# K and V of a batch in one 2 MB load each, in an attention kernel with grouped heads

## The chip, the cores and the metric

The kernel runs on one core of a Trainium2 chip. The metric is the device time of one execution in microseconds. The core's engines are TensorE (PE in the profile; PEld is its loading of weights), VectorE (DVE), ScalarE (ACT), GpSimd (POOL) and SyncE (SP). Each runs its own instructions in order, and they meet through semaphores. Loads from HBM into the on-chip memory (SBUF) are carried by 16 DMA engines; a load is given to them by one instruction on the queue of POOL or SP.

## The reference, cut to what matters

```python
B, Sq, D = 32, 4, 1024
Hq, Hkv, Sk, Dh = 32, 4, 2048, 128          # all bfloat16
q = (x @ wq).reshape(B, Sq, Hq, Dh).transpose(0, 2, 1, 3)
k = repeat(k_cache, 8, axis=1)               # k_cache, v_cache: [B, Hkv, Sk, Dh]
v = repeat(v_cache, 8, axis=1)
scores = einsum("bhqd,bhkd->bhqk", q, k) * Dh ** -0.5
o = einsum("bhqk,bhkd->bhqd", softmax(scores), v)
return o.transpose(0, 2, 1, 3).reshape(B, Sq, Hq * Dh) @ wo
```

Each batch has 2 MB of K and 2 MB of V (four groups of 512 KB each), and wq and wo are 8 MB each, so 151 MB are read in all. The 4 query rows of the 32 heads make 128 rows per batch, 32 for each group of heads that shares a K and a V.

## The kernel before, in words

All loads but that of x go through one ring of nine slots in SBUF, each of 2 MB (128 partitions by 16 KB). The order of the loads is the list `stream` (line 123): four slots of wq, K of batches 0 to 2, then V of batch b and K of batch b+3 in turn, at the end four slots of wo. POOL issues them in that order (lines 151 to 167, through `fetch`, line 144). Before it issues load n it waits until load n-9 has been used up (`freed`, line 133): a wq slot by its last projection matmul, a K slot by its last transposes, a V slot by its last PV matmul. Each slot is filled by four DMAs of 512 KB, each with a semaphore of its own; for K and V these are the four groups of heads. In a group, partition p holds 16 consecutive rows of the cache, which is one piece of 4 KB.

The work on a batch i goes through these steps; the line numbers are those of the profile:

- `kt` (line 236, copied out at lines 346 on DVE and 348 on ACT): K is transposed by TensorE, 64 transposes in eight fills f = 0 to 7 of eight transposes, two fills for each group. A fill goes to one of four PSUM buffers (ps_a, ps_b, ps_c, ps_o, in turn), waits for the load of its group g = f // 2 and for the buffer to have been copied out. DVE copies out five of the fills, ACT three.
- `qk` (line 281): 16 matmuls give the scores of 128 rows by 2048 keys.
- max and its negative (lines 372 and 373, DVE), exp with the row sums (line 401, ACT), the reciprocal `rinv` and a diagonal matrix of it (lines 381 and 382, DVE). On DVE, rinv and diag stand between the third and the fourth copy of the `kt` fills.
- `tr` (line 252): four fills of four matmuls transpose the probabilities and scale them by the diagonal; they use the same four PSUM buffers.
- `pv` (line 263): 64 matmuls with V; it waits for all four parts of V. Its result is copied out on DVE (`ot`, line 361).

TensorE runs them in a fixed order, with K transposed two batches ahead: for each i, qk(i), pv(i-1), kt(i+2), tr(i). After the last, pv(31) follows and then the output projection `oproj` (line 314): 64 matmuls over wo, in 16 pieces of four matmuls, each of which waits for its piece of 512 KB of wo; the first also for ot(31). Two copies (lines 391 and 411) and one store on SP end the kernel.

Of the kernel before, what the change touches and what calls it, by code (L numbers as in the profile page):

```python
# [54 lines left out]
def bass_standalone__gqa_block_cached__sampling_kernel(  # L55
# [9 lines left out]
    _, Hkv, Sk, Dh = k_cache.shape  # L65
# [6 lines left out]
    NKT = Sk // 128  # L72
    G = Hkv
# [16 lines left out]
    pr = Program()  # L90

    with ExitStack() as es:
# [40 lines left out]
        def freed(l):  # L133
            kind, i = l
            return {"wq": ("qproj", i), "k": ("kt", i, KT_FILLS - 1), "v": ("pv", i)}[kind]

        def slot(l):
            return slots[:, slot_of[l], :]
# [4 lines left out]
        def fetch(dst, src):  # L143
            return lambda e: e.dma_start(dst, src, single_packet=True)  # L144
# [6 lines left out]
        for n, l in enumerate(stream):  # L151
            kind, i = l
            waits = [freed(stream[n - NSLOT])] if n >= NSLOT else []
            s, v = f"slot{n % NSLOT}_", 16 * (n // NSLOT + 1)
            if kind == "wq":
                for q in range(G):
                    cols = slice(q * SLOT // G, (q + 1) * SLOT // G)
                    pr.load("pool", fetch(slot(l)[:, cols], wq_v[:, i, cols]), l + (q,), s + str(q), v, waits)
            elif kind in "kv":
                src = (k_cache if kind == "k" else v_cache)[i].rearrange("g (p t) d -> g p (t d)", p=128)  # L160
                for g in range(G):
                    pr.load("pool", fetch(slot(l)[:, g * NKT * Dh:(g + 1) * NKT * Dh], src[g]), l + (g,), s + str(g), v, waits)
            else:
                for q in range(WO_PARTS):
                    part = slot(l)[:, q * WO_PER * D:(q + 1) * WO_PER * D].rearrange("p (h n) -> p h n", n=D)
                    h0 = i * HPL + q * WO_PER
                    pr.load("pool", fetch(part, wo_v[:, h0:h0 + WO_PER, :]), ("wo", i, q), f"wo{i * WO_PARTS + q}", 16, waits)
# [296 lines left out]
```

## Time and profile before

| | |
|---|---|
| time, median of 3 runs (lowest to highest) | 388.26 us (388.24 to 388.43) |
| the profiled execution: its span, first to last instruction | 386.1 us |
| TensorE busy with matmuls; with loading weights | 293.4 us (76%); 238.9 us (62%) |
| DVE; ACT; POOL busy | 245.3 us (64%); 198.6 us (51%); 154.1 us (40%) |
| read from HBM | 151.26 MB, 392 GB/s over the span |
| mean granted clock of TensorE | 0.951 |
| longest chain of work, by share | DMA 83%, PE 7%, POOL 5%, ACT 2% |

The profiled execution has no other time of its own than the span; it lies 2.2 us under the median of the runs, which have what comes ahead of the first and after the last instruction as well.

The page divides the span into 40 slices and gives the busy tenths of each engine in each of them, the clock that TensorE was granted (PEclk, in tenths of full speed) and the rate of the DMA engines. The timeline has one row for a run of like instructions: its start, its length, the engine, the line, and what it works on; in brackets the idle time before it and what ended that. The part on DMA issues gives the median time from the issue of a load to its landing. The longest waits, in total over the kernel:

```profile
POOL slots L144 <- PE ps_o L263: 102.4, 28, 5.0
ACT pp_sb L401 <- DVE negmx L373: 93.0, 32, 3.8
POOL slots L144 <- PE ps_a L252: 68.6, 29, 5.3
PEld ps_o L263 <- issue: 53.6, 32, 2.7
DVE mx L372 <- PE ps_s L281: 38.6, 32, 1.6
PE ps_o L263 <- DMA slots<-in_v_cache_dram: 37.6, 28, 2.3
```

The columns are who waited for whom, us in total, how often, and the longest in us. TensorE's waits for K are in smaller rows, 18.8 us in all for both its matmuls and its weight loads.

### The profile page before, as it was taken

The numbers are of one execution on the slowest core, as the hardware profiler recorded it, in microseconds if no ns is written. First come the engines' busy times: TensorE is split into PE (matmuls) and PEld (weight loads), VectorE is DVE, ScalarE is ACT, GpSimd is POOL, SyncE is SP. The second block draws the span as 40 slices with busy tenths as digits, with TensorE's granted clock in tenths as the row PEclk, the third lists the DMA queues.
The fourth block names the chain that finished last, engine by engine and source line by source line (L and its number), as shares of the span: only waits on it lengthen the run. The fifth ranks groups of instructions, "written<-read, shape, count | busy, mean of one in ns | idle before, by whom it ended". The sixth has DMA issues, their size and how long they took to land.

```text
span 386.1 us, 12016 instructions
## 1 busy us (share of the span) xinstructions
PE 293.4 (76%) x5446; PEld 238.9 (62%) x5448; DVE 245.3 (64%) x390; ACT 198.6 (51%) x230; POOL 154.1 (40%) x294
## 2 busy tenths in 40 slices
PE   1969777878887877677978877787868778776596
PEld 0968556666766666465866766666756666664542
DVE  0017887777676777677677777686767766774400
ACT  1016666655564666456656455466564666654300
POOL 8975344433344443344443334443334436500000
PEclk9999999999898999999899899898989999997689
DMA  7999999999999999999999999999999999999982
GB/s 276 413 407 407 407 407 407 409 408 407 407 410 407 409 408 407 405 409 406 408 409 404 410 407 410 407 411 407 406 408 408 409 408 406 410 407 404 389 322 112
DMA packets 41810, 152.30 MB, mean 394 GB/s; under 512 B 4640, under 2 KB 4640, under 8 KB 41760
## 3 DMA queue, kind: packets, MB, share of 16 engines
q0 software_dynamic: 41472, 151.01, 98.5%
q8 instruction: 43, 0.70, 0.8%
q1 hardware_dynamic: 288, 0.52, 0.5%
q14 instruction: 7, 0.06, 0.0%
HBM read 151.26 MB, written 0.26 MB: 392 GB/s over the span
## 4 chain that ended last, share of the span: by engine, by line
DMA 83%; PE 7%; POOL 5%; ACT 2%; issue 1%; POOLq 0%; DVE 0%
DMA slots<-in_k_cache_dram 45%; DMA slots<-in_v_cache_dram 23%; DMA slots<-in_wo_dram 11%; POOL slots L144 5%; DMA slots<-in_wq_dram 4%; ACT KT_sb L348 2%; PE ps_o L263 2%; PE ps_c L236 1%; PE ps_o L236 1%; PE ps_a L236 1%; PE ps_s L281 1%; PE ps_s L211 0%; PE ps_b L236 0%; PE ps_s L314 0%; PE ps_o L252 0%
## 5 line engine op out<-in xcount | busy, mean ns | idle before, releaser
L401 ACT ACTIVATE pp_sb<-ps_s,negmx 128x2048 bf16<-128x2048 f32 x32 | 62.9, 1967 | 93.0 <-DVE negmx L373 93.0
L144 POOL DMA_DIRECT2D slots<-in_k_cache_dram x128 | 66.8, 529 | 100.1 <-PE ps_o L263 93.1
L372 DVE TENSOR_REDUCE mx<-ps_s 128x1 f32<-128x2048 f32 x32 | 73.3, 2291 | 38.6 <-PE ps_s L281 38.6
L144 POOL DMA_DIRECT2D slots<-in_v_cache_dram x128 | 66.9, 529 | 75.3 <-PE ps_a L252 66.0
L263 PEld LDWEIGHTS ps_o<-pp_sb,slots 128*128 128x128 bf16 x2048 | 54.4, 97 | 53.6 <-issue 53.6
L263 PE MATMUL ps_o<-pp_sb,slots 128*128 128x32 bf16 x2048 | 56.9, 179 | 38.6 <-DMA slots<-in_v_cache_dram 37.6
L348 ACT ACTIVATE KT_sb<-ps_a 128x1024 bf16<-128x1024 bf16 x32 | 32.7, 1022 | 34.8 <-PE ps_a L236 34.7
L236 PE MATMUL ps_c<-ident,slots 128*128 128x128 bf16 x512 | 40.9, 224 | 7.5 <-DMA slots<-in_k_cache_dram 5.5
L346 DVE COPY KT_sb<-ps_b 128x1024 bf16<-128x1024 bf16 x64 | 43.6, 682 | 1.2 <-PE ps_b L236 0.8
L236 PE MATMUL ps_a<-ident,slots 128*128 128x128 bf16 x512 | 42.1, 229 | 2.0 <-DVE KT_sb L346 1.4
L236 PE MATMUL ps_b<-ident,slots 128*128 128x128 bf16 x512 | 41.8, 228 | 0.0
L236 PE MATMUL ps_o<-ident,slots 128*128 128x128 bf16 x512 | 40.2, 222 | 2.0 <-DVE KT_sb L346 1.0
L236 PEld LDWEIGHTS ps_c<-ident,slots 128*128 128x128 bf16 x512 | 31.7, 101 | 11.1 <-DMA slots<-in_k_cache_dram 9.8
L348 ACT ACTIVATE KT_sb<-ps_c 128x1024 bf16<-128x1024 bf16 x32 | 32.7, 1022 | 8.4 <-PE ps_c L236 8.4
L236 PEld LDWEIGHTS ps_a<-ident,slots 128*128 128x128 bf16 x512 | 31.7, 102 | 6.0 <-DMA slots<-in_k_cache_dram 3.0
L236 PEld LDWEIGHTS ps_o<-ident,slots 128*128 128x128 bf16 x512 | 31.7, 99 | 4.4 <-DVE KT_sb L346 3.1
L281 PE MATMUL ps_s<-KT_sb,QT_sb 128*32 128x512 bf16 x512 | 34.3, 389 | 0.0
L236 PEld LDWEIGHTS ps_b<-ident,slots 128*128 128x128 bf16 x512 | 33.9, 103 | 0.1
L346 DVE CAST pp_sb<-ps_a 128x512 bf16<-128x512 f32 x32 | 22.1, 691 | 17.9 <-PE ps_a L252 17.9
L348 ACT ACTIVATE KT_sb<-ps_o 128x1024 bf16<-128x1024 bf16 x32 | 32.7, 1022 | 0.2 <-PE ps_o L236 0.2
L346 DVE COPY KT_sb<-ps_a 128x1024 bf16<-128x1024 bf16 x32 | 22.1, 690 | 7.9 <-PE ps_a L236 7.9
L252 PE MATMUL ps_o<-diag,pp_sb 128*128 128x128 bf16 x128 | 13.2, 227 | 15.3 <-ACT KT_sb L348 15.3
(50 smaller groups left out, 308.9 us busy)
## 6 DMA issues: line engine op xcount, KB each, us to landing
slots<-in_k_cache_dram POOLq DMA_DIRECT2D x128, 512.0 KB, 41.4
slots<-in_v_cache_dram POOLq DMA_DIRECT2D x128, 512.0 KB, 42.2
slots<-in_wq_dram POOLq DMA_DIRECT2D x16, 512.0 KB, 9.8
slots<-in_wo_dram POOLq DMA_DIRECT2D x16, 512.0 KB, 42.6
pp_sb<-in_x_dram SPq DMA_DIRECT2D x1, 256.0 KB, 2.6
out_dram<-pp_sb SPq DMA_DIRECT2D x1, 256.0 KB, 2.0
```

Source lines behind the costliest of these rows:

```text
L144: return lambda e: e.dma_start(dst, src, single_packet=True)
L236: ins = e.transpose(dst[:, q * 128:(q + 1) * 128], slot(("k", b))[:, (g * NKT + t) * Dh:(g * NKT + t + 1) * Dh], ident[:, :],)
L252: ins = e.matmul(dst[:, q * 128:(q + 1) * 128], lhsT=P_sb[:, t * 128:(t + 1) * 128], rhs=diag[:, b % 2, :], start=True, stop=True)
L263: ins = e.matmul(ps_o[:, 32 * g:32 * (g + 1)], lhsT=v[:, (g * NKT + t) * Dh:(g * NKT + t + 1) * Dh], rhs=PT_sb[:, t, 32 * g:32 * (g + 1)], ...
L281: ins = e.matmul(ps_s[32 * g:32 * (g + 1), c * 512:(c + 1) * 512], lhsT=QT_sb[:, i, REP * g:REP * (g + 1), :], rhs=KT_sb[:, i % 2, g, c * ...
L346: pr.op("dve", lambda e: e.tensor_copy(dst, src), w, ("evac",) + job)
L348: pr.op("act", lambda e: e.activation(dst, src, ACT.Copy), w, ("evac",) + job)
L372: pr.op("dve", lambda e, i=i: e.tensor_reduce(mx[:, i:i + 1], ps_s[:, :], AX.X, ALU.max), [("qk", i)], ("max", i))
L401: pr.op("act", lambda e, i=i: e.activation(P_sb, ps_s[:, :], ACT.Exp, bias=negmx[:, i:i + 1], scale=scale, accum_out=ssum[:, i:i + 1]), [( ...
```

## The change

K of a batch, and V of a batch, is loaded by one DMA: its access pattern has 128 partitions, four pieces of 4 KB in each, one for each group. In the cache the four pieces of a partition lie 512 KB apart; in SBUF they lie side by side, where they lay before. The load has one semaphore, and the names of the three other parts are set to the same event, so that whoever waited for a part waits for the whole. The loads of x, wq and wo, the order of the loads and all work on the engines stay.

```diff
             elif kind in "kv":
-                src = (k_cache if kind == "k" else v_cache)[i].rearrange("g (p t) d -> g p (t d)", p=128)
-                for g in range(G):
-                    pr.load("pool", fetch(slot(l)[:, g * NKT * Dh:(g + 1) * NKT * Dh], src[g]), l + (g,), s + str(g), v, waits)
+                src = (k_cache if kind == "k" else v_cache)[i].rearrange("g (p t) d -> p g (t d)", p=128)
+                dst = slot(l).rearrange("p (g n) -> p g n", g=G)
+                pr.load("pool", fetch(dst, src), l + (0,), s + "0", v, waits)
+                for g in range(1, G):
+                    pr.event[l + (g,)] = pr.event[l + (0,)]
             else:
```

## The prediction

> **What bounds the kernel now.** I read the page's 40 slices first, then the DMA queue over a quiet stretch (100 to 200 us), then the timeline of TensorE. The page has:
>
> ```profile
> PEclk9999999999898999999899899898989999997689
> DMA  7999999999999999999999999999999999999982
> GB/s 276 413 407 407 407 407 407 409 408 407 407 410 407 409 408 407 405 409 406 408 409 404 410 407 410 407 411 407 406 408 408 409 408 406 410 407 404 389 322 112
> ...
> slots<-in_k_cache_dram POOLq DMA_DIRECT2D x128, 512.0 KB, 41.4
> slots<-in_wo_dram POOLq DMA_DIRECT2D x16, 512.0 KB, 42.6
> ```
>
> The DMA engines are full from the second slice on, at 407 GB/s, and a load lands some 41 us after its issue: about eight of the nine slots are always queued. So the stream sets the pace, and a slot that comes free a few us later stops nothing. The queue in the quiet stretch:
>
> ```profile
> DMA packets 11155, 40.78 MB, mean 408 GB/s; under 512 B 1238, under 2 KB 1238, under 8 KB 11142
> ```
>
> There is one small record (the 4-byte write that counts a DMA as landed) to every eight of 4 KB. Of the trace's packet records I compared start times: within one DMA the 4 KB records of an engine begin 159 ns apart, and after a 4-byte record the next data begins 6 ns later, not 159. 8 x 159 + 6 = 1.28 us is also the distance at which loads land one after another. Nothing else lies between two DMAs: they are already back to back.
>
> Last, what is late. TensorE through an early batch whose data had all arrived, and from the last K (batch 31) to the end:
>
> ```profile
> 48.95 0.61 PE L236 MATMUL ps_a<-ident,slots 128*128 128x128 bf16 x8
> ...
> 52.25 0.62 PE L236 MATMUL ps_c<-ident,slots 128*128 128x128 bf16 x8 [0.21 <-DVE rinv L381]
> 53.16 0.62 PE L236 MATMUL ps_o<-ident,slots 128*128 128x128 bf16 x8 [0.30 <-DVE KT_sb L346]
> ...
> 55.23 1.05 PE L281 MATMUL ps_s<-KT_sb,QT_sb 128*32 128x512 bf16 x16
> ```
>
> ```profile
> 341.19 0.61 PE L236 MATMUL ps_a<-ident,slots 128*128 128x128 bf16 x8
> ...
> 344.43 0.62 PE L236 MATMUL ps_c<-ident,slots 128*128 128x128 bf16 x8 [0.23 <-DMA slots<-in_k_cache_dram]
> ...
> 347.40 1.05 PE L281 MATMUL ps_s<-KT_sb,QT_sb 128*32 128x512 bf16 x16
> 349.81 1.75 PE L263 MATMUL ps_o<-pp_sb,slots 128*128 128x32 bf16 x64 [1.36 <-DMA slots<-in_v_cache_dram]
> 353.71 0.59 PE L252 MATMUL ps_a<-diag,pp_sb 128*128 128x128 bf16 x4 [2.15 <-DVE diag L382]
> ...
> 355.50 1.90 PE L281 MATMUL ps_s<-KT_sb,QT_sb 128*32 128x512 bf16 x16
> ...
> 365.30 1.87 PE L263 MATMUL ps_o<-pp_sb,slots 128*128 128x32 bf16 x64 [0.78 <-ACT pp_sb L348]
> 368.02 13.59 PE L314 MATMUL ps_s<-slots,oT_sb 128*128 128x512 bf16 x58 [0.85 <-DVE oT_sb L361]
> 381.85 1.04 PE L314 MATMUL ps_s<-slots,oT_sb 128*128 128x512 bf16 x4 [0.24 <-DMA slots<-in_wo_dram]
> ```
>
> Read the last two rows first. The output projection (L314) runs without a pause from 368.02 until the last piece of wo, for which it waits 0.24 us; by the 0.215 us between its matmuls those four would have begun at 381.45, so it waits 0.4 us in all. **The end therefore has two bounds 0.4 us apart**: the last landing, and a serial chain: K31 landed, its transposes (L236), tr(29), qk(30) at 347.40, max, exp, tr(30), qk(31), max, exp, tr(31), pv(31), projection. No other load comes between to hold that chain: V29 (349.81) only fills the wait for max and exp.
>
> **What the change does, part by part.** The order of instructions on POOL shows 64 copies of 128x4x2048 in place of 256 of 128x2048, at the same places; the other engines keep theirs.
>
> 1. *Small records.* Three of four go, for 64 K and V loads: 64 x 3 x 6 ns = 1.15 us per engine at the end of V, and 61 x 3 x 6 ns = 1.1 us by K31, the 61st of these loads. Bounds: 0 (hidden), and by the records' own duration of 9 ns, 1.73 us. I take 6 ns, read off the starts.
>
> 2. *Issue.* POOL spends 528 ns on a load of 128 pieces and 716 on one of wo with 256, so 188 more per 128: an estimate of 528 + 3 x 188 = 1.1 us for 512 pieces (bounds 0.53 and 4 x 0.53 = 2.1). The 41 us of queue hide it; without that cover it would be some 1 us a slot.
>
> 3. *Rate of the copies.* The trace has no DMA of four pieces per partition, 512 KB apart. Bounds: wo, in two pieces per partition, ran at 390 GB/s from 356 to 366 us, 4.4% under 408; K and V take 134 MB / 408 = 329 us, so +14.5 us. On the other side a record of 8 KB took 307 ns at the start (427 GB/s on 16 engines): -15 us. The pieces stay 4 KB, so the nearest row is K and V themselves: no change. wq, whose partitions lie 64 KB apart and not 4, also ran at 408 GB/s (12 to 25 us), which speaks against any price of distance.
>
> The Trainium skill speaks against this part: "DMA: Bandwidth & Descriptors", section "Latency and other measured facts", has copies with rows 512 KiB apart at 207 GB/s against 214 in full. By that 3.3%, 329 us would be 11 us longer, near 399 us; no run here shows rows so far apart. The same page's "Rules for kernel authors" asks for 1 MiB and more per DMA, and its "Bandwidth" gives 78% of the peak at 1 MB; here 512 KB loads already follow each other with 6 ns between, so that rule has nothing to win.
>
> 4. *The wait.* Today the transposes of group 0 start when 512 KB have landed; now all eight fills wait for the whole 2 MB. Behind them on TensorE, in order, stand tr(i), qk(i+1) and pv(i). V loses nothing: pv already waits for all four parts.
> In the middle of the kernel it costs nothing. With its data there, a K takes 6.28 us from first fill to the next qk (48.95 to 55.23), 0.5 of it waits behind rinv (0.21 + 0.30) that exp will by then have met: 5.8. With qk (1.0) and pv (1.8) that is 8.6 us from a K's landing to the next idle, and Ks land 10.2 us apart. The new wait stands for the old ones (1.4 for V, 0.4 for K), 1.6 us idle remain, and slots come free some 3 to 4 us later against a lead of 41.
> At the end it has no cover. K31 is complete at 344.4; by then six of eight fills are done and qk(30) starts 3.0 us later. Now qk(30) starts 5.8 us after the landing: +2.8. The landing is 1.1 us earlier: +1.7 for qk(30) and, as all behind it is serial, for the projection's start. 0.4 of this is the projection's present wait: **+1.3 us** at the end. The last landing moves to -1.15 and no longer decides.
>
> Sum against the profiled execution: span 386.1 + 1.3 = 387.4. The median of the runs is 388.26, 2.2 above that span; I carry the difference over: 389.6 us.
>
> **The rivals.**
>
> *A, the clock also falls (391.2).* Half clock comes after idle: after 1.96 us of waiting ahead of 183.41 the fills from 185.01 took 0.85 us each and not 0.45, and qk came at 192.37, 7.4 after the first fill; after 1.4 us (349.81 has 1.36) it mostly did not. The new idle of 1.6 us lies between. If K31 falls on it: 7.4 - 5.8 = 1.6 more.
>
> *B, the chain is partly swallowed (388.3, between 387.5 and 389.0).* From 352.3 to 359.1 and from 362.5 to 369.3 the granted clock is 0.50: qk(31) takes 1.90 and not 1.05, eight tr fills 0.43 apart and not 0.22, the projection's first three matmuls 0.43: 0.85 + 1.6 + 0.65 = 3.1 us are lost. A chain shifted by 1.7 us meets these stretches elsewhere and may lose 1 us or so less; it may as well lose more, so this isn't the likeliest.
>
> *C, faster (387.1).* The stream still decides, and the 1.15 us of small records are the whole result. Place: the last wo landing; price -1.15; it decides once the projection starts at least 0.75 us earlier than now, that is if the chain loses 2.4 us less than I reckon (most of B's 3.1, or faster transposes). For it: the DMA row is full throughout and the margin today is on its side; against it: only 0.4 us of margin.
>
> *D, the copies' rate moves* by more than the small records, either way within the +14.5 and -15 us above, mostly within 4 of them. For it: an untried form of copy. Against: 4 KB pieces at one rate for K, V and wq.
>
> That the change does not do what it says is excluded by the order on POOL.
>
> **How the numbers follow.** Forecast 0.42 (own range 388.9 to 390.5, the bounds of the small records and 6.28 in place of 5.8); A 0.16; B 0.17; C 0.15; D slower 0.06, D faster 0.04. About 0.2%, 0.78 us, is what a measurement of this kernel can tell from no change. Slower by more: the forecast without its lower edge, A and D slower, 0.62. Within: B and that edge, 0.19. Faster: C and D faster, 0.19. The range takes in C and A: 387.0 to 391.8; D's two ends (0.10) stay outside, with a little of A.
>
> **What would show it.** Small records 98 x 16 = 1,568 in place of 4,640, and GB/s up by some 0.35%. No row of L236 starting before the whole K has landed; one TensorE wait of about 1.6 us per batch, for K, and almost none for V. Issue to landing still about 40 us. At the end qk(30) about 5.8 us after K31 lands, and the projection running through without a wait for wo. I am wrong if the projection still waits for wo at its end (C), if the quiet stretch leaves 405 to 412 GB/s (D), or if POOL's lead is gone.

## The result, and the profile after

The changed kernel took 390.93 us (median of 4 runs, 390.80 to 391.60), the kernel before 388.35 us (388.24 to 388.62): 1.0068 times as long, 95% interval 1.0054 to 1.0082, so 2.6 us slower. The forecast was 389.6 us, range 387.0 to 391.8. In a second set of runs on another occasion the changed kernel took 390.63 us (389.24 to 392.14), ratio 1.0059, interval 1.0037 to 1.0080. The profiled execution of the changed kernel, one of the first set, took 390.99 us with a span of 389.2 us, 3.1 above the span of the one before.

First the page of the changed kernel, the rows that answer to those shown of before:

```profile
PEclk9999999898999998969999989999898999998679
DMA  7999999999999999999999999999999999999961
...
slots<-in_k_cache_dram POOLq DMA_DIRECT2D x32, 2048.0 KB, 42.3
slots<-in_wo_dram POOLq DMA_DIRECT2D x16, 512.0 KB, 41.0
```

and the queue over the same quiet stretch, 100 to 200 us:

```profile
DMA packets 10227, 40.77 MB, mean 408 GB/s; under 512 B 312, under 2 KB 312, under 8 KB 10213
```

The DMA engines are as full as before and the lead of some 41 us is still there. Three quarters of the small records are gone, 312 in place of 1,238 in these 100 us. But the rate is the same 408 GB/s: the stream won nothing by it.

The waits of the changed kernel, who for whom, us in total, how often, longest:

```profile
PEld ps_a L238 <- DMA slots<-in_k_cache_dram: 47.8, 30, 3.4
PE ps_a L238 <- DMA slots<-in_k_cache_dram: 44.2, 30, 3.3
```

TensorE's 37.6 us of waits for V are gone from the list, and it waits 44.2 us for K, 1.5 us in each of 30 batches. (The lines of the changed kernel lie two further down: L238 is L236 of before, L283 is L281, L316 is L314.) The end, from TensorE's timeline:

```profile
344.57 0.62 PE L238 MATMUL ps_a<-ident,slots 128*128 128x128 bf16 x8 [1.78 <-DMA slots<-in_k_cache_dram]
...
350.26 1.05 PE L283 MATMUL ps_s<-KT_sb,QT_sb 128*32 128x512 bf16 x16
351.24 1.76 PE L265 MATMUL ps_o<-pp_sb,slots 128*128 128x32 bf16 x64
356.56 0.38 PE L254 MATMUL ps_a<-diag,pp_sb 128*128 128x128 bf16 x4 [3.56 <-DVE diag L384]
...
358.09 1.90 PE L283 MATMUL ps_s<-KT_sb,QT_sb 128*32 128x512 bf16 x16
...
367.90 1.87 PE L265 MATMUL ps_o<-pp_sb,slots 128*128 128x32 bf16 x64 [0.78 <-ACT pp_sb L350]
370.24 15.79 PE L316 MATMUL ps_s<-slots,oT_sb 128*128 128x512 bf16 x64 [0.47 <-DVE oT_sb L363]
```

No fill of K31 begins before the whole 2 MB has landed, at 344.5. qk(30) begins 5.7 us after that, at 350.26; it was 347.40. The projection then runs through all its 64 matmuls without a wait for wo: the last piece of wo lands at 382.6, the projection ends at 386.03. Before, it ended at 382.89, one microsecond after its last piece. **The end has changed from the stream to the chain of work behind K31.**

The stretches of the end by clock (columns: stretch, its length, busy time of PE, PEld, DVE, ACT and POOL with the number of instructions, granted clock, DMA share, GB/s):

```profile
356.90:360.30 3.40, 3.40 (x43) 1.83 (x41) 1.64 (x3) 1.19 (x2) 0.00 (x0) 0.50 1.02 395
360.30:363.70 3.40, 1.42 (x57) 1.31 (x53) 2.39 (x3) 1.14 (x1) 0.00 (x0) 1.00 1.03 387
363.70:373.90 10.20, 7.39 (x89) 4.73 (x90) 2.10 (x5) 2.11 (x4) 0.00 (x0) 0.50 0.98 369
```

The last stretch at clock 0.50 holds the first 3.7 us of the projection; before it held 1.7 us of it (367.6, where its first weights are loaded, to 369.3). At half clock a matmul of the projection takes 0.43 us and not 0.215, so a stretch of half clock costs half its length: 1.8 against 0.9 us.

### The profile page after: what moved, and what is told of

Read it like the earlier page. It is cut to its first block, busy times and chain, and to the rows that moved or that the text cites. A ratio compares the mean times of both kernels' runs of the same rounds, so it can differ in the third digit from the quotient of the medians.

```text
span 389.2 us, 11695 instructions
## 1 busy us (share of the span) xinstructions
PE 295.6 (76%) x5448; PEld 245.9 (63%) x5448; DVE 242.2 (62%) x390; ACT 196.4 (50%) x230; POOL 67.8 (17%) x102
## 4 chain that ended last, share of the span: by engine, by line
DMA 68%; PE 19%; ACT 8%; DVE 3%; issue 1%; POOL 1%; POOLq 0%
DMA slots<-in_k_cache_dram 66%; ACT KT_sb L350 6%; PE ps_s L316 4%; PE ps_o L265 3%; PE ps_s L283 3%; DVE mx L374 2%; ACT pp_sb L403 2%; PE ps_a L238 2%; DMA slots<-in_wq_dram 2%; PE ps_b L238 1%; PE ps_s L213 1%; PE ps_c L238 1%; PE ps_o L254 1%; PE ps_o L238 1%; POOL slots L144 0%
## 5 line engine op out<-in xcount | busy, mean ns | idle before, releaser
L238 PE MATMUL ps_a<-ident,slots 128*128 128x128 bf16 x512 | 43.3, 233 | 45.1 <-DMA slots<-in_k_cache_dram 44.2
L238 PEld LDWEIGHTS ps_a<-ident,slots 128*128 128x128 bf16 x512 | 33.3, 105 | 49.0 <-DMA slots<-in_k_cache_dram 47.8
L265 PEld LDWEIGHTS ps_o<-pp_sb,slots 128*128 128x128 bf16 x2048 | 53.5, 96 | 14.6 <-issue 13.7
L144 POOL DMA_DIRECT2D slots<-in_v_cache_dram x32 | 23.7, 741 | 159.4 <-PE ps_a L254 126.7
L238 PE MATMUL ps_o<-ident,slots 128*128 128x128 bf16 x512 | 42.2, 229 | 8.0 <-DVE KT_sb L348 8.0
L238 PE MATMUL ps_b<-ident,slots 128*128 128x128 bf16 x512 | 42.9, 232 | 0.0
L238 PE MATMUL ps_c<-ident,slots 128*128 128x128 bf16 x512 | 42.7, 231 | 0.0
L144 POOL DMA_DIRECT2D slots<-in_k_cache_dram x32 | 23.7, 741 | 102.1 <-PE ps_o L265 90.6
L238 PEld LDWEIGHTS ps_o<-ident,slots 128*128 128x128 bf16 x512 | 33.0, 103 | 12.0 <-DVE KT_sb L348 11.8
L238 PEld LDWEIGHTS ps_b<-ident,slots 128*128 128x128 bf16 x512 | 34.8, 105 | 0.4 <-DVE KT_sb L348 0.2
L238 PEld LDWEIGHTS ps_c<-ident,slots 128*128 128x128 bf16 x512 | 34.3, 104 | 0.5
L283 PE MATMUL ps_s<-KT_sb,QT_sb 128*32 128x512 bf16 x512 | 34.3, 389 | 0.0
```

Source lines behind the costliest of these rows:

```text
L238: ins = e.transpose(dst[:, q * 128:(q + 1) * 128], slot(("k", b))[:, (g * NKT + t) * Dh:(g * NKT + t + 1) * Dh], ident[:, :],)
L265: ins = e.matmul(ps_o[:, 32 * g:32 * (g + 1)], lhsT=v[:, (g * NKT + t) * Dh:(g * NKT + t + 1) * Dh], rhs=PT_sb[:, t, 32 * g:32 * (g + 1)], ...
L283: ins = e.matmul(ps_s[32 * g:32 * (g + 1), c * 512:(c + 1) * 512], lhsT=QT_sb[:, i, REP * g:REP * (g + 1), :], rhs=KT_sb[:, i % 2, g, c * ...
```

## The experiments

The theory: the loss is the wait for the whole of K near the end, where no idle time takes it up; the form of the loads, and the wait in all earlier batches, cost nothing. Rival 1: the form of the copies slows the stream (in the first profile K31 and the last piece of wo landed 0.15 and 0.78 us later than before). Rival 2: each batch adds a little. The table has all runs; qk(30) is its start in the profiled execution, which stands for the lateness of the chain. Each ratio is to the runs of the kernel before of the same set, whose medians go from 388.31 to 388.43 us.

| kernel | time, us (runs) | ratio to before, 95% interval | qk(30) at |
|---|---|---|---|
| before | 388.35 | | 347.40 |
| changed | 390.93 (4) | 1.0068 [1.0054, 1.0082] | 350.26 |
| changed, again (e7) | 390.63 (6) | 1.0059 [1.0037, 1.0080] | 349.94 |
| V in one load, K in four (e1) | 388.32 (11) | 1.0001 [0.9993, 1.0010] | 347.65 |
| four loads, every fill waits for the whole K (e3) | 391.08 (5) | 1.0065 [1.0053, 1.0077] | 350.33 |
| the same for K31 only (e4) | 391.85 (4) | 1.0094 [1.0079, 1.0108] | 352.60 |
| the same, TensorE kept awake before K31 (e9) | 390.52 (5) | 1.0053 [1.0040, 1.0066] | 350.04 |
| changed, but K31 in four (e2) | 389.91 (12) | 1.0038 [1.0026, 1.0049] | 349.00 |
| changed, but K30 and K31 in four (e8) | 389.02 (12) | 1.0016 [1.0004, 1.0029] | 349.81 |
| changed, but K28 to K31 in four (e10) | 388.39 (11) | 1.0003 [0.9993, 1.0012] | 347.72 |
| changed, TensorE kept awake at the end (e5) | 388.52 (12) | 0.9999 [0.9991, 1.0008] | 350.29 |
| before, TensorE kept awake at the end (e6) | 388.34 (11) | 0.9996 [0.9987, 1.0004] | 347.27 |

### V alone in the new form (e1)

```diff
+                if kind == "k":
+                    (four loads of 512 KB, as in the kernel before)
+                else:
+                    (one load of 2 MB, as in the changed kernel)
```

Brackets stand for code that is left out. Here and in e2, e8 and e10 the counts that the loads' semaphores must reach are added up load by load, as the loads of one slot no longer have one form.

> V of a batch by one load of 2 MB, K by four of 512 KB as before. Theory (the loss is the wait for the whole K31 at the end; the form of the loads and the waits of the other batches cost nothing): the time of the kernel before, 388.3 us, within 0.4. Rival 1 (the form of the copies costs the stream something: the last landing came at 382.58 and not 381.80 us): half of the loads have the new form, so half of that, 388.7 us, with the chain unharmed. Rival 2 (the loss is collected a little in every batch by the wait for the whole K and the clock behind it): 388.3 us, as K is waited for by groups.

388.32 us, ratio 1.0001. V in one load costs nothing, and rival 1 finds no half of a loss here. Its last piece of wo landed at 382.41, later than in the profile before (381.80), and its time is that of before all the same.

### The wait alone (e3)

```diff
-            pr.op("pe", fn, [("k", b, g)] + ring_waits(job), job)
+            pr.op("pe", fn, [("k", b, gg) for gg in range(G)] + ring_waits(job), job)
```

> The loads of the kernel before, four of 512 KB for each K and V, but every fill of the K transposes waits for all four groups. The wait alone, without the change of the loads. Theory: the time of the changed kernel, 390.9 us, within 0.4. Rival 1: 390.1 us, since the last landing and K31 come as early as before. Rival 2: 390.9 us. A gain in the stream from fewer small records (1.15 us by my prediction) would show as this run being slower than the changed kernel by about 1 us.

391.08 us, the time of the changed kernel, with the loads of the kernel before. Rival 1 falls: the wait gives the whole loss. It is not 1 us slower than the changed kernel either, so the small records that go are worth nothing that shows.

### The wait in the last batch alone, and the clock (e4, e9)

```diff
-            pr.op("pe", fn, [("k", b, g)] + ring_waits(job), job)
+            pr.op("pe", fn, [("k", b, gg) for gg in (range(G) if b == B - 1 else [g])] + ring_waits(job), job)
```

> The kernel before, but the fills of the last K alone wait for all four of its groups; the 31 others wait by group as before. Theory: 390.9 us, within 0.5, all of the loss from one wait in one batch. Rival 1: 390.1 us. Rival 2: 388.4 us, one thirty-second of the loss.

391.85 us, the slowest of all, with one wait in one batch. Rival 2 falls, and so does a part of the theory, which had 390.9. The timeline of this kernel shows what is added:

```profile
344.79 1.01 PE L236 MATMUL ps_a<-ident,slots 128*128 128x128 bf16 x8 [3.15 <-DMA slots<-in_k_cache_dram]
345.60 1.06 PE L236 MATMUL ps_b<-ident,slots 128*128 128x128 bf16 x8
...
350.08 0.61 PE L236 MATMUL ps_o<-ident,slots 128*128 128x128 bf16 x8
...
352.60 0.61 PE L281 MATMUL ps_s<-KT_sb,QT_sb 128*32 128x512 bf16 x8
```

As the other batches run early here, TensorE has waited 3.15 us when K31 is complete, not 1.78, and the fills that follow come 0.85 us apart and not 0.45. From 342.5 to 349.3 us the granted clock was 0.50. qk(30) comes 7.8 us after the first fill. That is what rival A of the prediction describes, though A spoke of the changed kernel, whose fills of K31 ran at full clock in its profile. To test it, TensorE was kept busy through that wait with transposes that nobody reads:

```diff
+            if i + AHEAD == B - 1:
+                warm(46, [("evac", "tr", i - 1, 0)])     # 46 transposes of ident into ps_a
             if i + AHEAD < B:
                 for f in range(KT_FILLS):
                     kt_fill(i + AHEAD, f)
```

> The kernel before with the fills of K31 alone waiting for all four groups, and 46 transposes of the identity, which nobody reads, in TensorE's idle time ahead of them. Without these the time was 391.85 us: after 3.15 us of waiting the fills ran at half clock and qk(30) came 7.8 us after the first of them. If the half clock is what makes this run slower than the changed kernel: qk(30) 5.7 us after the first fill, and 390.6 us (390.2 to 391.2), about the changed kernel's time. If not: 391.8 us.

390.52 us. In the timeline the fills follow at full clock and qk(30) comes 5.7 us after the first:

```profile
341.08 2.73 PE L298 MATMUL ps_a<-ident 128*128 128x128 bf16 x46
344.38 0.61 PE L236 MATMUL ps_a<-ident,slots 128*128 128x128 bf16 x8 [0.56 <-DMA slots<-in_k_cache_dram]
...
350.04 1.05 PE L281 MATMUL ps_s<-KT_sb,QT_sb 128*32 128x512 bf16 x16
```

So the half clock made 1.3 us of the 3.5 us of e4, and the wait in the last batch alone, without it, costs 2.2 us (390.52 against 388.34 in the same set of runs).

### The last K by groups again (e2, e8, e10)

All K and V in one load, except K of the last one, two or four batches:

```diff
+                if kind == "k" and i >= B - 2:           # e8; B - 4 in e10; in e2: if l == ("k", B - 1):
+                    (four loads of 512 KB)
+                else:
+                    (one load of 2 MB)
```

> All K and V by one load of 2 MB each, but K of the last batch by four of 512 KB. Theory: 388.3 us, within 0.4, the same as before, as qk(30) starts about 3.0 us after K31 has landed and no longer 5.7. Rival 1 (form of the copies): 389.1 us, as 63 of the 64 loads have the new form and the last landing stays 0.8 us late. Rival 2 (collected in every batch): 390.8 us, as 31 of 32 batches still wait for the whole.

389.91 us (388.40 to 391.05), which meets none of the three expectations. What I had left out shows in the timeline of e2: its first fill of K31, then qk(30).

```profile
342.72 0.61 PE L249 MATMUL ps_a<-ident,slots 128*128 128x128 bf16 x8
...
349.00 1.05 PE L294 MATMUL ps_s<-KT_sb,QT_sb 128*32 128x512 bf16 x16
```

K31's groups were there, but TensorE came to them at 342.72 and not at 341.19: it was still late from K30, for whose whole it had waited. Against the kernel before, qk(29) is 3.0 us late (340.13 and 337.17) and qk(30) still 1.6: lateness is handed on, and worked off only as far as a batch has idle time.

> All K and V by one load of 2 MB, but K of the last two batches by four of 512 KB. With only K31 in four parts the time was 389.91 us: K30, still whole, left TensorE late, and its transposes of K31 began at 342.72 and not at 341.19. If lateness is handed on like this and worked off at some 1.6 us a batch, the second batch removes the rest: 388.4 us (388.0 to 388.8), with qk(30) at about 347.5. If the form of the other 62 loads costs anything, or each batch adds its share for good: 389.5 us or more.

389.02 us (387.88 to 390.35), somewhat over half of the way that was left. The runs fall in two heaps, five from 387.88 to 388.32 and seven from 388.71 up. The profiled one is of the upper heap (389.67 us). In it the first fills of K29, which was still waited for whole, come 0.85 us apart (from 323.8 to 327.2 us the granted clock was 0.52), and TensorE paused twice without a releaser in the profile:

```profile
323.86 1.04 PE L249 MATMUL ps_a<-ident,slots 128*128 128x128 bf16 x8 [1.68 <-DMA slots<-in_k_cache_dram]
324.68 1.06 PE L249 MATMUL ps_b<-ident,slots 128*128 128x128 bf16 x8
...
338.08 0.49 PE L249 MATMUL ps_c<-ident,slots 128*128 128x128 bf16 x6 [1.05 <-issue]
...
352.62 0.55 PE L276 MATMUL ps_o<-pp_sb,slots 128*128 128x32 bf16 x16 [0.46 <-issue]
```

Against the kernel before, qk(28) is 4.1 us late, of which the half clock made some 1.2 (in the changed kernel, at full clock there, it is 2.9 us late); qk(29) is 3.8 us late, as a batch works off about 1.4 us and the first pause adds 1.05; qk(30) is 2.4 us late. With the idle time used up by the lateness of K29, such a pause goes straight through to the end. The second pause lies in pv(29), which only fills the wait for max and exp. The kernel before has such pauses too (three of 0.6 to 0.9 us in its K transposes) and takes them up. All five end 1.4 to 1.6 us after a packet of 16 KB of the row "q8 instruction" has been moved, so TensorE probably waited for its next instructions; no run tests that. Whether the other runs of the upper heap had a half clock or a pause there was not seen; only one execution is profiled.

> All K and V by one load of 2 MB, but K of the last four batches by four of 512 KB. Two such batches gave 389.02 us, spread from 387.88 to 390.35; in the profiled execution TensorE, still late from K29, also lost 1.05 us in a pause within the transposes of K30. If lateness is only handed on and worked off, four batches are enough whatever a pause costs: 388.4 us (388.1 to 388.7), spread like the kernel before, with qk(30) at about 347.5. If the form of the other 60 loads costs the rest: about 389.0 us again.

388.39 us, ratio 1.0003: with four batches by group all is paid back, though 60 of the 64 loads have the new form. TensorE is back to waiting for groups of K and for V:

```profile
334.31 0.62 PE L249 MATMUL ps_c<-ident,slots 128*128 128x128 bf16 x8 [0.22 <-DMA slots<-in_k_cache_dram]
...
347.72 1.05 PE L294 MATMUL ps_s<-KT_sb,QT_sb 128*32 128x512 bf16 x16
349.62 1.77 PE L276 MATMUL ps_o<-pp_sb,slots 128*128 128x32 bf16 x64 [0.86 <-DMA slots<-in_v_cache_dram]
...
382.49 1.04 PE L327 MATMUL ps_s<-slots,oT_sb 128*128 128x512 bf16 x4 [0.24 <-DMA slots<-in_wo_dram]
```

### The clock at the end (e5, e6, and e7 beside them)

```diff
+            if i == B - 2:
+                warm(58, [("evac", "tr", i - 1, 0)])     # 34 in e6
+            if i == B - 1:
+                warm(56, [("evac", "tr", i - 1, 0)])
             for f in range(TR_FILLS):
                 tr_fill(i, f)
+        warm(6, [("evac", "tr", B - 1, 0)])
         pv(B - 1)
+        warm(6, [])
```

> The changed kernel with transposes of the identity, which nobody reads, in TensorE's idle time of the last two batches: 58 before tr(30), 56 before tr(31), 6 before pv(31), 6 before the projection. It tests the share of the granted clock in the last chain. If the half clock behind idle time is part of the loss: the chain wins back tr(30) 0.6, qk(31) 0.85, tr(31) 0.8 and the projection's 1.8 us, some 4 us in all, until the last landing of wo decides again: 388.5 us (387.9 to 389.2). If the clock has no part in it: 390.9 us or a little more, for the added work.

> The kernel before with the same filling of the idle time (34 transposes before tr(30), the rest alike). Theory: its end is the last landing of wo, 0.4 us after the chain could have been done, so a faster chain wins nothing: 388.3 us, at most 0.2 less. If the chain decides there too: about 3 us less, 385.3 us.

> The changed kernel once more, beside the two others on the same chip: 390.9 us (390.6 to 391.5) by every theory; what it tells is whether K31 and the last piece of wo again land late (K31 0.15, wo 0.78 us later than in the kernel before), as rival 1 (form of the copies) has it, or whether that differs from one execution to the next.

The changed kernel kept awake takes 388.52 us, the time of the kernel before. Its timeline:

```profile
350.29 1.05 PE L283 MATMUL ps_s<-KT_sb,QT_sb 128*32 128x512 bf16 x16
...
357.58 1.05 PE L283 MATMUL ps_s<-KT_sb,QT_sb 128*32 128x512 bf16 x16
...
368.32 11.39 PE L330 MATMUL ps_s<-slots,oT_sb 128*128 128x512 bf16 x50 [0.35 <-DVE oT_sb L377]
...
382.52 1.04 PE L330 MATMUL ps_s<-slots,oT_sb 128*128 128x512 bf16 x4 [0.24 <-DMA slots<-in_wo_dram]
```

qk(30) is as late as in the changed kernel, 350.29, but qk(31) takes 1.05 us and not 1.90, the projection starts 1.9 us sooner, runs at full clock, and waits for the last piece of wo again. The lateness is still there; the chain is merely fast enough to hide it. The kernel before kept awake takes 388.34 us, ratio 0.9996: its projection waits 0.25 us for each of its last nine pieces of wo, and nothing is won, as the stream decides. So no version here beats the kernel before, whose bound is the stream of 151 MB.

In e7 K31 landed at 344.2 and the last wo at 381.9; with the old loads it was 344.5 and 382.1 in e3, and 344.7 and 382.6 in e4. So the late landings of the first profile differ from one execution to the next and do not belong to the form of the loads.

## Why the forecast of 389.6 was right in kind and too small

- **Small records (part 1): wrong.** 1.1 us by K31 were expected; the landing of K31 moved by +0.15. On the engine that is first done with each load, a slot of 2 MB takes 5.105 us before and 5.108 after, averaged over the 63 steps from K0 to V31. The 6 ns between the starts of records were seen rightly, but they are not time of the stream: without them the engine moves no more. What sets its 1.28 us per 512 KB was not tried. Rival C, a gain from these records alone, falls with them.
- **Issue (part 2): right.** A load of 512 pieces takes POOL 741 ns (1.1 us expected, bounds 0.53 to 2.1), and the lead hides it: 42 us from issue to landing.
- **Rate (part 3): right.** 408 GB/s in the quiet stretch before and after, with pieces 512 KB apart. The Trainium skill's figure for rows 512 KiB apart ("DMA: Bandwidth & Descriptors", "Latency and other measured facts") is for copies between HBM tensors with that distance from partition to partition. The prediction's estimate of 11 us from it does not carry over to this load into SBUF, whose partitions lie 4 KB apart and only the four pieces of each 512 KB. Rival D falls.
- **The wait (part 4): right in place and size.** 5.7 us from landing to qk(30) (5.8 expected), idle time of 1.5 to 1.8 us a batch (1.6). What was too narrow was "at the end": e2 and e8 show that the lateness of the batches ahead of it counts too.
- **The margin: right.** The projection's 0.4 us of waiting is gone.
- **The clock (rivals A and B): mis-sized.** I carried qk(30)'s shift unchanged to the end and gave the clock only as rivals, A at the fills of K31 and B as a gain. The fills ran at full clock in the profiled execution; the clock cost 0.9 us in the projection instead. That the measured 390.93 us lies near rival A's 391.2 is chance as far as that execution shows. Two of the six runs of e7 took 392.1 us, at mean clocks of 0.926 and 0.934, the two lowest of the changed kernel's ten runs; whether A happened in them was not seen.

The sum, by the profiled executions: K31's landing +0.15, from there to qk(30) 5.73 in place of 3.02, +2.71; from qk(30) to the projection -0.26 (the projection's first weights are loaded at 367.61 before and 370.21 after; tr(30) began at full clock); wait for wo -0.4; half clock in the projection +0.9. That is +3.1 us, as the spans differ. Expected were -1.1, +2.8, -0.4: +1.3. So the missing part is 1.2 us that the stream did not win and some 0.7 us of clock; the medians of the runs, 2.6 apart, are 0.5 us nearer than these two executions; the profiled span of before, 386.1 us, is the shortest of all runs of that kernel (median 386.5).

The Trainium skill has the clock's rule, "TensorE: Matmul & The Clock Gate", Part 1: half speed after an idle window of some 3.4 us, full speed after a busy one, the windows running free of the program. The rows agree with lengths of 3.4 us and multiples of it (356.9 to 360.3, 363.7 to 373.9) and with a phase that changes between runs; but the 3.4 us before the clock fell need not be idle throughout. In e4 it fell at 342.5, only 0.9 us into the wait of 3.15, and the 3.4 us ahead held a pv of 1.75 us; in the kernel before it fell at 185.0, and the 3.4 us ahead held a pv of 1.76 us.

## What to carry to other kernels

A load that is waited for in parts is also a way to start work early: before parts are merged, look for the place where the work behind the last of them has no idle time, which is the end, and count what runs serially from there; what the last batches ahead of it lose is handed on to it. In a full queue the number of DMAs cost nothing here; look whether loads already land back to back before expecting a gain from larger ones. And where a serial chain decides the end, keep TensorE's clock in the sum: idle time ahead of it doubled the time of what followed.

## What the runs showed of the hardware

The 16 DMA engines do not finish together. The changed kernel from 340 to 386 us, rate in 40 slices of 1.15 us:

```profile
GB/s 410 392 402 410 417 410 410 392 406 413 406 392 403 399 392 395 395 388 385 388 392 385 388 385 388 388 378 399 296 239 232 199 203 207 196 50 29 0 0 0
```

The last piece of wo is complete only at 382.6. By the counts of its semaphore the first engine had finished with it at 373.1, half of the engines by 376.1, and the other half only from 380.5 on. The lag between first and last engine grows from 0.8 us with the first loads to 9.5 us, in steps: the completion of successive slots is 5.1 us apart, but six times 6.6, so 1.5 us is lost at each step. Instructions come through the same engines, 42 fetches of 16 KB (0.69 MB in the page's row "q8 instruction"). The six loads that are late were under way at the 1st, 9th, 17th, 25th, 33rd and 41st of these fetches, which makes the fetches the likely cause; a run with fewer instructions was not made.
